# Three small parameter loads moved from GpSimd's queue to SyncE's, with three pairs of later loads merged

## The chip, the cores and the metric

The kernel runs on one core of a Trainium2 chip. The time is the device time of one execution in microseconds (us), as a median of several executions. The profile shows one execution in detail; its span, from the first recorded instruction to the last, is about 2 us shorter than the time.

Names used below: PE is the matmul engine, DVE the vector engine, ACT the scalar engine, POOL is GpSimd, SP is SyncE, which in this kernel does nothing but issue DMAs. SPq is SyncE's queue of issues.

## The reference, cut to what matters

```python
xn  = layernorm(x)                         # x: (1, 2048, 512), bf16
dt  = exp(log_dt)                          # 512 values each: log_dt, Lambda_re, Lambda_im
Lam_bar = exp(dt * (Lambda_re + 1j * Lambda_im))
ssm = scan over t of h = Lam_bar * h + B_bar xn[t], then 2 Re(C h) + xn * Dskip
glu = (silu(xn @ w1) * (xn @ w3)) @ w2     # w1, w3: 512 x 1792, w2: 1792 x 512
out = x + ssm + glu
```

The three parameter vectors, 512 bf16 values (1 KB) each, are the subject of the change.

## The kernel before

The 2048 rows of x are worked on in four blocks of 512. Of block 0 the normalised rows are transposed on PE; of blocks 1 to 3 by DMA transposes from SBUF to SBUF. The 14 gate tiles (128 columns of w1 and of w3 each) of block 0 begin as soon as the first weights are there. All weights, the x blocks and the transposes go through SyncE's queue in one order.

```python
    for c in range(2):                                         # x chunks 0 and 1, half each
        for eng, dsl in ((nc.sync, slice(0, D // 2)), (nc.scalar, slice(D // 2, D))):
            eng.dma_start(out=x_blk[0][:, c, dsl], in_=xv[:, c, dsl])
    nc.scalar.dma_start(out=x_blk[0][:, 3, :], in_=xv[:, 3, :])
    nc.sync.dma_start(out=x_blk[0][:, 2, :], in_=xv[:, 2, :])
    load_w(0, 2 * P)                                           # w1, then w3: gate tiles 0 and 1
    load_w(2 * P, 4 * P)                                       # tiles 2 and 3
    for i, src in enumerate((A_log_dt, A_Lambda_re, A_Lambda_im)):
        nc.gpsimd.dma_start(out=par_rows[i * NPT:(i + 1) * NPT, :], in_=src.rearrange("(t p) -> t p", p=P))

    def bulk_loads():
        ...                                                    # cut: one ACT write that holds the next load back
        load_w(4 * P, MID * P)                                 # tiles 4 to 7
        load_x(1)
        nc.sync.dma_start_transpose(out=bt_re, in_=A_B_re)
        nc.sync.dma_start_transpose(out=bt_im, in_=A_B_im)
        load_w(MID * P, 11 * P)
        load_w(11 * P, F)
        nc.sync.dma_start_transpose(out=ct_re, in_=A_C_re)
        nc.sync.dma_start_transpose(out=ct_im, in_=A_C_im)
        nc.sync.dma_start(out=w2_sb, in_=B_w2.rearrange("(t p) d -> p t d", p=P))    # 1.8 MB
        nc.sync.dma_start(out=dskip_row, in_=A_Dskip.partition_broadcast(P))
```

After these, SyncE issues block 1's four transposes (`xnT<-xn`), which PE needs when it begins block 1, near 39 us. Then come the loads of x blocks 2 and 3 (`late_loads`).

On PE the start of block 0 reads, shortened:

```python
            quarter(0, (0, 1), 2)      # 16 small matmuls: rows 0-127, tiles 0 and 1 (needs the first weight pair)
            pps = params_transpose()   # needs par_rows
            ...
            quarter(1, (0, 1))
            ln_first_transpose(2)
            quarter(0, (2,))           # needs the second weight pair
```

The loads from SyncE and ACT use eight completion semaphores in turn: the instruction listing shows each load, from the ninth on, waiting for the completion of the load eight places before it.

Of the kernel before, what the change touches and what calls it, by code (L numbers as in the profile page):

```python
# [16 lines left out]
P = 128  # L17
# [34 lines left out]
def kernel(  # L52
# [17 lines left out]
    nc = tc.nc  # L70
    _, S, D = A_x.shape
    F = B_w1.shape[1]
# [6 lines left out]
    NPT = PS // P  # L79
# [3 lines left out]
    MID = 8  # L83
# [30 lines left out]
    par_rows = const.tile([3 * NPT, P], BF16, name="par_rows")  # L114
# [15 lines left out]
    def load_w(f0, f1, eng1=nc.sync, eng3=nc.sync):  # L130
        eng1.dma_start(out=w1_sb[:, :, f0:f1], in_=w1v[:, :, f0:f1])  # L131
        eng3.dma_start(out=w3_sb[:, :, f0:f1], in_=w3v[:, :, f0:f1])

    def load_x(b, parts=1):
        n = CPB // parts
        for i in range(0, CPB, n):
            nc.sync.dma_start(out=x_blk[b][:, i:i + n, :], in_=xv[:, b * CPB + i:b * CPB + i + n, :])
# [4 lines left out]
    nc.scalar.dma_start(out=x_blk[0][:, 3, :], in_=xv[:, 3, :])  # L142
    nc.sync.dma_start(out=x_blk[0][:, 2, :], in_=xv[:, 2, :])  # L143
    load_w(0, 2 * P)
    load_w(2 * P, 4 * P)
    for i, src in enumerate((A_log_dt, A_Lambda_re, A_Lambda_im)):
        nc.gpsimd.dma_start(out=par_rows[i * NPT:(i + 1) * NPT, :], in_=src.rearrange("(t p) -> t p", p=P))

    def bulk_loads():
        nc.scalar.activation(out=w1_sb[:, 0, 4 * P:4 * P + 1], in_=rstd_all[:, 0:1], func=ACT.Copy)  # L150
        load_w(4 * P, MID * P)
        load_x(1)
        nc.sync.dma_start_transpose(out=bt_re, in_=A_B_re)
        nc.sync.dma_start_transpose(out=bt_im, in_=A_B_im)
        load_w(MID * P, 11 * P)
        load_w(11 * P, F)
        nc.sync.dma_start_transpose(out=ct_re, in_=A_C_re)
        nc.sync.dma_start_transpose(out=ct_im, in_=A_C_im)
        nc.sync.dma_start(out=w2_sb, in_=B_w2.rearrange("(t p) d -> p t d", p=P))
        nc.sync.dma_start(out=dskip_row, in_=A_Dskip.partition_broadcast(P))  # L160

    def late_loads():
        load_x(2)
        load_x(3, 2)


    ones = nc.const_aps.tensor(1.0, (P, TBLK), BF16)
# [276 lines left out]
    def glu(b):  # L444
# [25 lines left out]
        if b == 0:  # L470
# [13 lines left out]
            ln_stats(0, 0)  # L484
            ln_first_rstd(0)
            bulk_loads()
            ln_stats(0, 1)
            ln_first_rstd(1)
# [121 lines left out]
    bg.flush(("ln", 1))  # L610
    gate()
    late_loads()
    finish_c = [weight_c(pt) for pt in range(NPT)]
    res_tasks(0)
# [53 lines left out]
```

## Time and profile before

| | before |
|---|---|
| time, median of 6 runs | 213.28 us (212.97 to 214.24) |
| span of the profiled run | 211.6 us |
| PE busy | 207.6 us, 98% |
| granted PE clock | 0.999 |
| PE waits for the first w3 load until | 6.98 us |
| PE gap before block 1 | 0.22 us, until 39.40 us |

From the page of the kernel before, parts 1 and 4. The first line is busy time with its share and the number of instructions; the second is the chain of waits by engine.

```profile
PE 207.6 (98%) x1075; PEld 99.2 (47%) x1075; DVE 155.8 (74%) x186; ACT 116.5 (55%) x221; POOL 24.7 (12%) x50
...
PE 94%; DMA 2%; ACT 1%; SPq 1%; issue 0%; DVE 0%
```

PE bounds the kernel: only some 4 us of the span are not PE. A change of loads can win only where PE waits for a load.

From the timeline of the kernel before. The columns are start and duration in us, engine, line, operation, output and input, and count; the bracket is the idle time of the engine just before, and what ended it. These lines stand in order of time.

```profile
1.26 0.80 POOL L147 DMA_DIRECT2D par_rows<-in_A_log_dt_dram  x1 [0.83 <-POOLq L652]
2.60 0.51 SPq L132 DMA_DIRECT2D w_sb<-in_B_w_dram  x1
3.15 0.52 SPq L131 DMA_DIRECT2D w_sb<-in_B_w_dram  x1
3.72 0.51 SPq L132 DMA_DIRECT2D w_sb<-in_B_w_dram  x1
6.92 6.05 SPq L153 DMA_TRANSPOSE bt_re<-in_A_B_re_dram  x1
6.98 0.95 PE L481 MATMUL gu_ps<-xnT,w_sb 128*128 128x128 bf16 x14 [0.26 <-DMA w_sb<-in_B_w_dram]
9.11 0.61 PE L481 MATMUL bu_ps<-xnT,w_sb 128*128 128x128 bf16 x8
12.90 8.80 PE L451 MATMUL gu_ps<-xnT,w_sb 128*128 128x512 bf16 x40
27.46 9.25 SPq L223 DMA_TRANSPOSE xnT<-xn  x4
39.40 10.95 PE L451 MATMUL gu_ps<-xnT,w_sb 128*128 128x512 bf16 x50 [0.22 <-issue]
```

Read it so: the first w3 load is issued at 2.60, the second weight pair at 3.15 and 3.72. PE goes on at 6.98, when the first w3 load has landed. At 9.11 PE uses the second pair. Block 1's transposes are issued from 27.46 on, and PE begins block 1 at 39.40 after a short gap. The two gaps after the warm-up, 0.26 and 0.22 us, are all that the loads cost PE here.

### The profile page before, as it was taken

To read this page: it belongs to the slowest core of one execution; us is meant where nothing else is said; L and a number is where in the kernel's file an instruction comes from. 1 tells how busy PE (TensorE), PEld (TensorE's weight loads), DVE (VectorE), ACT (ScalarE), POOL (GpSimd) and SP (SyncE) were. 2 spreads that over 40 slices of the span, in tenths; PEclk is the share of its full clock that TensorE was granted. 3 is DMA by queue.
4 is the path that set the end of the run, shared out by engine and by line. 5 is a ranking of instruction groups with operands and counts; after the bars stand their busy time and mean duration, and the time that the engine had idled before them with its cause. 6 is when DMAs were issued, how large, how long until landed. Compare 5 with 4: busy or idle time off the path is not lost.

```text
span 211.6 us, 2823 instructions
## 1 busy us (share of the span) xinstructions
PE 207.6 (98%) x1075; PEld 99.2 (47%) x1075; DVE 155.8 (74%) x186; ACT 116.5 (55%) x221; POOL 24.7 (12%) x50
## 2 busy tenths in 40 slices
PE   8999999999999999999999999999999999999994
PEld 2864444444444444444444444444444444444464
DVE  4789799999918969899999897827999991121111
ACT  4699787699866864066666786036666630000000
POOL 7350299200000020000000012000000000000000
PEclk9999999999999999999999999999999999999999
DMA  5999999800000003500000001510000000100110
GB/s 160 326 237 283 251 297 166 248 0 0 0 3 0 0 0 77 99 25 0 0 0 5 0 0 25 124 50 3 0 2 0 3 0 0 50 25 28 36 40 25
DMA packets 27245, 13.68 MB, mean 65 GB/s; under 512 B 15840, under 2 KB 27232, under 8 KB 27232
## 3 DMA queue, kind: packets, MB, share of 16 engines
q1 hardware_dynamic: 26560, 13.21, 26.9%
q10 hardware_dynamic: 576, 0.30, 0.5%
q8 instruction: 8, 0.13, 0.2%
q14 instruction: 5, 0.04, 0.1%
q0 software_dynamic: 96, 0.00, 0.0%
HBM read 7.74 MB, written 2.10 MB: 46 GB/s over the span
## 4 chain that ended last, share of the span: by engine, by line
PE 94%; DMA 2%; ACT 1%; SPq 1%; issue 0%; DVE 0%
PE gu_ps L451 43%; PE y_ps L556 23%; PE y_ps L562 13%; PE bu_ps L379 12%; DMA w_sb<-in_B_w_dram 2%; PE gu_ps L481 2%; PE bu_ps L481 1%; ACT u L381 1%; SPq L141 0%; ACT tabe L346 0%; PE y_ps L219 0%; SPq L131 0%; SPq L143 0%; DVE o L567 0%; PE y_ps L280 0%
## 5 line engine op out<-in xcount | busy, mean ns | idle before, releaser
L451 PE MATMUL gu_ps<-xnT,w_sb 128*128 128x512 bf16 x424 | 92.3, 379 | 0.2 <-issue 0.2
L451 PEld LDWEIGHTS <-w_sb 128*128 128x128 bf16 x424 | 41.3, 98 | 50.3 <-issue 0.7
L556 PE MATMUL y_ps<-w_sb,hgT 128*128 128x512 bf16 (+2 forms) x252 | 50.4, 356 | 0.0
L461 ACT ACTIVATE u<-gu_ps 128x512 bf16<-128x512 f32 x55 | 33.2, 603 | 11.6 <-PE gu_ps L451 11.2
L460 ACT ACTIVATE g<-gu_ps 128x512 bf16<-128x512 f32 x55 | 33.1, 602 | 9.7 <-PE gu_ps L451 9.5
L567 DVE TENSOR_TENSOR o<-y_ps,xn 128x512 bf16<-128x512 f32 (+2 forms) x18 | 11.3, 629 | 35.8 <-PE y_ps L562 35.8
L556 PEld LDWEIGHTS <-hgT 128*128 128x128 bf16 x252 | 23.6, 98 | 25.2
L381 ACT ACTIVATE u<-bu_ps 128x512 bf16<-128x512 f32 x32 | 19.1, 597 | 24.5 <-PE bu_ps L379 24.5
L415 DVE TENSOR_TENSOR_SCAN u<-rho,h,u 128x512 bf16<-128x512 f32 x24 | 29.5, 1270 | 0.2
L467 DVE TENSOR_TENSOR hgT<-g,u 128x1024 bf16<-128x1024 bf16 x28 | 19.0, 682 | 6.6 <-ACT u L461 6.6
L562 PEld LDWEIGHTS <-h 128*128 128x128 bf16 x144 | 13.5, 98 | 14.3
L562 PE MATMUL y_ps<-ct_re,h 128*128 128x512 bf16 (+2 forms) x72 | 16.8, 356 | 0.0
L562 PE MATMUL y_ps<-ct_im,h 128*128 128x512 bf16 (+2 forms) x72 | 16.8, 356 | 0.0
L379 PE MATMUL bu_ps<-xnT,bt_re 128*128 128x512 bf16 x64 | 16.4, 379 | 0.1
L379 PE MATMUL bu_ps<-xnT,bt_im 128*128 128x512 bf16 x64 | 16.4, 379 | 0.0
L402 DVE TENSOR_TENSOR p<-u,tabe 128x2048 bf16<-128x2048 bf16 x8 | 9.8, 1222 | 3.5 <-ACT u L381 3.4
L252 POOL TENSOR_SCALAR acc<-acc 128x4 f32<-128x4 f32 x2 | 1.0, 497 | 80.8 <-ACT xn L251 80.8
L420 DVE TENSOR_TENSOR p<-u,tabe 128x2048 bf16<-128x2048 bf16 x8 | 9.8, 1224 | 0.2
L427 DVE TENSOR_TENSOR h<-h,p 128x2048 bf16<-128x2048 bf16 x8 | 9.8, 1223 | 0.2
L405 DVE TENSOR_TENSOR u<-u,tabe 128x2048 bf16<-128x2048 bf16 x8 | 9.8, 1222 | 0.2
L409 DVE TENSOR_TENSOR u<-u,p 128x2048 bf16<-128x2048 bf16 x8 | 9.8, 1224 | 0.1
L379 PEld LDWEIGHTS <-bt_re 128*128 128x128 bf16 x64 | 6.2, 98 | 7.8 <-issue 0.3
(92 smaller groups left out, 148.5 us busy)
## 6 DMA issues: line engine op xcount, KB each, us to landing
out_dram<-o SPq DMA_DIRECT2D x15, 128.0 KB, 1.7
w_sb<-in_B_w_dram SPq DMA_DIRECT2D x1, 1792.0 KB, 10.8
w_sb<-in_B_w_dram SPq DMA_DIRECT2D x4, 384.0 KB, 4.8
w_sb<-in_B_w_dram SPq DMA_DIRECT2D x4, 256.0 KB, 4.5
w_sb<-in_B_w_dram SPq DMA_DIRECT2D x2, 512.0 KB, 5.9
x_blk<-in_A_x_dram SPq DMA_DIRECT2D x2, 512.0 KB, 6.1
x_blk<-in_A_x_dram SPq DMA_DIRECT2D x2, 256.0 KB, 4.8
xnT<-xn SPq DMA_TRANSPOSE x12, 2.5
```

Source lines behind the costliest of these rows:

```text
L379: nc.tensor.matmul(out=ps, lhsT=bt[:, dt, pt * P:(pt + 1) * P], rhs=xnT_blk[b][:, dt, :], start=(dt == 0), stop=(dt == NDT - 1))
L381: nc.scalar.activation(out=u[:, j, ri, :], in_=ps, func=ACT.Copy)
L402: nc.vector.tensor_tensor(out=st["p"], in0=st["g"], in1=tabe[:, psl, 1:3, :], op=ALU.mult)
L405: nc.vector.tensor_tensor(out=st["g"], in0=st["g"], in1=tabe[:, psl, 0:1, :].to_broadcast(FULL), op=ALU.mult)
L415: nc.vector.tensor_tensor_scan(out=v, data0=rho[:, pt:pt + 1].to_broadcast([P, TBLK]), data1=v, initial=init, op0=ALU.mult, op1=ALU.add)
L451: nc.tensor.matmul(out=ps[:, tsl], lhsT=w[:, dt, f * P:(f + 1) * P], rhs=xnT[:, dt, tsl], start=(dt == 0), stop=(dt == NDT - 1))
L460: nc.scalar.activation(out=g16[:, f % 2, :], in_=g_ps, func=ACT.Silu)
L461: nc.scalar.activation(out=u16[:, f % 2, :], in_=u_ps, func=ACT.Copy)
L467: nc.vector.tensor_tensor(out=hgT[:, f - 1:f + 1, :], in0=g16, in1=u16, op=ALU.mult)
L556: nc.tensor.matmul(out=tiles[cl][:, dsl], lhsT=hg_blk[b][:, f, cl * P:(cl + 1) * P], rhs=w2_sb[:, f, dsl], start=(f == 0), stop=False)
L562: nc.tensor.matmul(out=tiles[cl][:, dsl], lhsT=h_blk[b][:, pt, ri, cl * P:(cl + 1) * P], rhs=ct[:, pt, dsl], start=False, stop=(ri == 1 an ...
L567: nc.vector.tensor_tensor(out=o[:, dsl], in0=tiles[cl][:, dsl], in1=xn_blk[b][:, cl, dsl], op=ALU.add)
```

## The change

The intent, as I read it, is to take GpSimd out of the loading and to let the parameters follow the weights that PE needs first. To keep the number of loads on SyncE, and with it the turns of the semaphores further on, four weight loads of 384 KB become two of 768 KB, and the two halves of x block 3 become one load.

```diff
     load_w(0, 2 * P)
+    for i, src in enumerate((A_log_dt, A_Lambda_re, A_Lambda_im)):
+        nc.sync.dma_start(out=par_rows[i * NPT:(i + 1) * NPT, :], in_=src.rearrange("(t p) -> t p", p=P))
     load_w(2 * P, 4 * P)
-    for i, src in enumerate((A_log_dt, A_Lambda_re, A_Lambda_im)):
-        nc.gpsimd.dma_start(out=par_rows[i * NPT:(i + 1) * NPT, :], in_=src.rearrange("(t p) -> t p", p=P))
 ...
-        load_w(MID * P, 11 * P)
-        load_w(11 * P, F)
+        load_w(MID * P, F)
 ...
-        load_x(3, 2)
+        load_x(3)
```

## The prediction

> **What bounds the kernel.** TensorE. The page of the kernel before has PE busy 207.6 of 211.6 us at a granted clock of 0.999; the chain of waits gives PE 94%, DMA 2%, ACT 1%. In the chain, the head is x and weight issues on SyncE until 2.60, then one DMA (the w3 half of gate tiles 0 and 1, 4.34 us to landing) until 6.94, then PE almost without a break to 208.9. In the timeline PE's gaps after its warm-up are 0.26 us at 6.7 (waiting for that w3 load) and 0.22 us at 39.2 (named "issue"; the fourth x transpose of block 1, issued near 35.5 and 3.6 us to landing, arrives near 39.1, so I take it for that). Together 0.48 us, 0.2% of the span: all that a change of loads can win in the middle.
>
> **What the change does.** The instruction listing shows PE, DVE and ACT with the same instructions in the same order.
> - Removed: three GpSimd issues (0.80, 0.53, 0.52 us, 1.26 to 3.10 in the timeline). GpSimd's constants come about 1.8 us earlier; nothing waits for them (ident is ready at 3.7, first used at 5.05).
> - Added: three SyncE issues behind the first weight pair, about 0.4 us each (x issues there took 0.40). The weights of tiles 2 and 3 then leave not at 3.15 and 3.72 but near 4.4 and, as the semaphores of these loads are handed round in turn and its slot now waits for the fourth x chunk (1.65 + 3.7 = 5.35), near 5.4. The w3 load of tiles 4 to 7 now waits for the first w1 load (landed 6.0), block 1's x for the first w3 load (6.9).
> - Also in the diff: four weight loads of 384 KB become two of 768 KB (two issues of about 0.5 us fewer, rows of 1536 B instead of 768 B), and two x loads become one.
>
> **What of it is critical.** The DMA engines are full from 2.5 us (9 tenths in every slice to 34 us, about 310 GB/s). At 4.4 us only about 0.55 of the first 1.05 MB has moved, so a later issue leaves no bubble: the tile-2 weights still land at about 8 to 8.8 us (before 7.65 and 8.7) and are wanted at 9.1. The first w3 load has less traffic mixed in and may land 0.2 to 0.5 us sooner, worth at most 0.26 us. The Trainium skill, "DMA: Bandwidth & Descriptors", "Issuing engines are not separate DMA queues", says that all queues run on the same 16 engines and a second issuer only saves issue time. Here that time is not on PE's path. The parameter rows now queue behind the weights and land near 7; PE wants them at 7.87, or near 7.6 if the head shortens: tight but probably no stall. Longer weight rows may bring block 1's transposes forward enough to close the 0.22 us gap.
>
> Sum: -0.25 (head) -0.15 (gap at 39) +0.1 (risk of a stall for tile 2's weights or the parameters) = -0.3 us.
>
> **Predicted:** 213.1 us, 80% range 212.4 to 214.0. Faster by over 2%: 0.01; within 2%: 0.98; slower by over 2%: 0.01.
>
> **What would show it.** Right: parameter issues on SyncE at 3.2 to 4.4; tile-2 weights issued near 4.4 and 5.4 yet landing before 9; PE's gaps at 6.7 and 39.2 smaller; PE busy 207 to 208. Wrong: PE waiting on DMA before the parameter transpose, or on w_sb at about 9 us; block 1's transposes landing later than 39.1.
>
> **What would make it wrong.** Small loads costing SyncE far more than 0.4 us each, or landing after 8 us; the semaphore waits leaving the DMA engines empty at 5 to 7 us, pushing every later load by 1 us or more. Even that costs 1 to 2 us, under 2%.

## More of the kernel before

From the windows view of the kernel before (columns: window, its length, PE busy time with number of instructions, granted clock, busy share of the DMA engines, GB/s moved):

```profile
5.50:7.00 1.50, 1.24 (x13) 1.00 1.14 310
7.00:13.00 6.00, 6.00 (x104) 1.00 1.14 318
13.00:24.00 11.00, 11.00 (x54) 1.00 1.12 259
```

## The result, and the profile after

Ratios are computed as the mean time of one kernel's runs over that of the other's in the same rounds, so they are not quite the ratio of the medians quoted. Executions over 1.5% slower than the fastest of the same kernel are left out of the means.

| | before | after |
|---|---|---|
| first comparison, medians of 6 and 6 runs | 213.28 us | 213.33 us (213.15 to 213.72) |
| ratio, 95% interval | | 1.0001 (0.9978 to 1.0023) |
| second comparison, one chip, 11 and 5 fast runs | 213.62 us | 213.49 us |
| ratio, 95% interval | | 0.9989 (0.9972 to 1.0007) |
| span of the profiled run | 211.6 us | 211.5 us |

The second comparison is the run e0_after_again below (its median with the slow run is 213.57 us). Both intervals contain 1: whatever the change does is smaller than about 0.3%.

The timeline of the changed kernel, the same places (its line numbers are one lower from the merged load on):

```profile
2.58 0.51 SPq L132 DMA_DIRECT2D w_sb<-in_B_w_dram  x1
3.13 0.45 SPq L146 DMA_DIRECT2D par_rows<-in_A_log_dt_dram  x1
3.62 0.26 SPq L146 DMA_DIRECT2D par_rows<-in_A_Lambda_re_dram  x1
3.93 0.29 SPq L146 DMA_DIRECT2D par_rows<-in_A_Lambda_im_dram  x1
4.27 0.40 SPq L131 DMA_DIRECT2D w_sb<-in_B_w_dram  x1
5.19 0.39 SPq L132 DMA_DIRECT2D w_sb<-in_B_w_dram  x1
6.69 0.95 PE L480 MATMUL gu_ps<-xnT,w_sb 128*128 128x128 bf16 x14 [0.30 <-DMA w_sb<-in_B_w_dram]
7.69 7.08 SPq L153 DMA_TRANSPOSE bt_re<-in_A_B_re_dram  x1
8.82 0.72 PE L480 MATMUL bu_ps<-xnT,w_sb 128*128 128x128 bf16 x8
12.72 8.80 PE L450 MATMUL gu_ps<-xnT,w_sb 128*128 128x512 bf16 x39
29.01 8.40 SPq L222 DMA_TRANSPOSE xnT<-xn  x4
39.32 10.95 PE L450 MATMUL gu_ps<-xnT,w_sb 128*128 128x512 bf16 x49 [0.33 <-DMA xnT<-xn]
```

PE goes on 0.29 us earlier after the first w3 load (6.69 against 6.98). The next line, eight matmuls on tile 2, takes 0.72 instead of 0.61 us: here PE waits for the second weight pair, which left later. At 12.72 it is still 0.18 us ahead. But block 1's transposes are issued 1.55 us later (29.01 against 27.46), and the gap before block 1 is larger, so that at 39.32 only 0.08 us of the lead is left. The last of the four, the one that PE waits for, landed only 0.12 us later than before (39.19 against 39.07 us), but PE now wanted it 0.2 us sooner. Most of the late issue is there as soon as SyncE is done with the transpose of bt_re, whose issue began 0.77 us later and took 7.08 instead of 6.05 us. In the chain of waits of the changed kernel the link before block 1 is no longer PE, but the fourth transpose:

```profile
36.20 2.99 DMA xnT<-xn
39.19 0.14 issue
39.32 2.75 PE gu_ps L450 x12
```

The windows view of the changed kernel:

```profile
5.50:7.00 1.50, 1.20 (x18) 1.00 0.84 219
7.00:13.00 6.00, 6.00 (x102) 1.00 1.12 310
13.00:24.00 11.00, 10.89 (x51) 1.00 1.14 235
```

The DMA engines move 219 GB/s between 5.5 and 7 us where they moved 310, and they do not make it up by 24 us. Rate difference times length gives about 0.14, 0.05 and 0.26 MB less for the three windows: the larger part is lost after 13 us, not in the dip. PE busy reads 206.4 us on this page against 207.6, but its trace holds 1057 matmul records instead of 1075, so that difference is one of missing records and says nothing.

### The profile page after: what moved, and what is told of

It reads as the page before. It is cut to its first block, busy times and chain, and to the rows that moved or that the text cites. A ratio compares the mean times of both kernels' runs of the same rounds, so it can differ in the third digit from the quotient of the medians.

```text
span 211.5 us, 2800 instructions
## 1 busy us (share of the span) xinstructions
PE 206.4 (98%) x1057; PEld 99.0 (47%) x1075; DVE 155.8 (74%) x186; ACT 116.5 (55%) x221; POOL 22.8 (11%) x47
## 4 chain that ended last, share of the span: by engine, by line
PE 81%; DVE 8%; ACT 3%; DMA 3%; SPq 1%; issue 1%; POOL 1%; DVEq 0%
PE gu_ps L450 34%; PE y_ps L555 23%; PE y_ps L561 13%; PE bu_ps L378 10%; DVE u L414 2%; DMA w_sb<-in_B_w_dram 2%; DMA xnT<-xn 1%; ACT g L459 1%; DVE stats L194 1%; ACT u L460 1%; PE gu_ps L480 1%; DVE hgT L466 1%; DVE xn L199 1%; ACT L510 1%; DVE u L408 1%
## 5 line engine op out<-in xcount | busy, mean ns | idle before, releaser
L378 PEld LDWEIGHTS <-bt_im 128*128 128x128 bf16 x64 | 6.3, 98 | 7.5
```

What stands on the lines that cost most here:

```text
L378: nc.tensor.matmul(out=ps, lhsT=bt[:, dt, pt * P:(pt + 1) * P], rhs=xnT_blk[b][:, dt, :], start=(dt == 0), stop=(dt == NDT - 1))
```

## The experiments

Four theories were to be told apart about the head, A or B for the earlier first weights, C or D for the lower DMA rate:

- A: the first w3 load lands earlier because the second weight pair, now later, is not mixed in with it.
- B: it lands earlier because the three GpSimd loads are gone.
- C: the small four-row loads hold up the DMA engines that serve them.
- D: the second pair's later issue leaves the DMA queue thin.

And one about the end: the arrival of block 1's transposes takes back what the head wins.

### e1_move_only: the move without the merges (one look)

```diff
     load_w(0, 2 * P)
+    for i, src in ...: nc.sync.dma_start(out=par_rows[...], ...)
     load_w(2 * P, 4 * P)
-    for i, src in ...: nc.gpsimd.dma_start(out=par_rows[...], ...)
```

> Only the parameter loads move to SyncE; the weight and x loads stay unmerged. If the move alone makes the changes seen in the head (both theories), the head is that of the changed kernel: first w3 load landed and PE going again at 6.7 us (before 6.98), DMA rate 5.5 to 7 us near 190 to 235 GB/s (before 306 to 312), the last load of block 1's transposes landing at 39.2 us or later. Two weight issues more than the changed kernel, so ct_re is issued about 1 us later than its 19.1 us, and the PE gap at 39 us is 0.33 us or up to 1 us more. If the merges hurt the queue instead, it is issued at or before 19 us.

The DMA rate from 5.5 to 7 us was 254 GB/s, above the expected range but well below the kernel before. The first weights came without a visible stop (16 matmuls in one group from 6.43 us). The ct_re load was issued at 20.44 us and the gap before block 1 was 1.14 us. So in this look the move alone goes with the dip and the late queue; the merges are not needed for either. How much they pay back is the question of the timed run further down.

### e3_params_second: parameters on SyncE behind the second weight pair (one look)

```diff
     load_w(0, 2 * P)
-    for i, src in ...: nc.sync.dma_start(out=par_rows[...], ...)
     load_w(2 * P, 4 * P)
+    for i, src in ...: nc.sync.dma_start(out=par_rows[...], ...)
```

> Parameter loads on SyncE, but behind the second weight pair. Theory A (the later weight pair makes the first w3 load land earlier, because less traffic is mixed in): the pair leaves at 3.1 and 3.7 again, so PE goes on at about 6.95 us as before. Theory B (the three GpSimd loads themselves had slowed the first weights): 6.7 us as in the changed kernel. Theory C (four-row loads in SyncE's rings hold up the DMA engines that serve them): the dip of the DMA rate (to about 200 GB/s) appears again, but later, about 6.5 to 8.5 us; theory D (the dip comes from the weight pair's late issue): no dip, 300 GB/s or more. Parameter rows land later, at 8 us or after, and PE waits for them before the parameter transpose (0 us before, up to 1 us now).

From its windows and its timeline:

```profile
5.50:7.00 1.50, 0.99 (x15) 1.00 1.13 338
...
6.88 0.95 PE L480 MATMUL gu_ps<-xnT,w_sb 128*128 128x128 bf16 x14 [0.51 <-DMA w_sb<-in_B_w_dram]
9.27 0.16 PE L279 MATMUL y_ps<-ident,par_rows 12*128 12x12 bf16 x1 [1.44 <-DMA par_rows<-in_A_Lambda_im_dram]
```

With the small loads on SyncE but the weight pair early, the rate stays at 338 GB/s, and from 7 to 13 us it is 316 GB/s. It sags to 297 and 266 GB/s in the half windows at 7.0 and 7.5 us (before: 300 and 296), which is not the dip to about 200 that C asked for: C is not borne out, D stands. But block 1's transposes were issued at 28.61 us, about 1.1 us later than before, without the dip: the low rate is not the only way to a late queue. PE went on at 6.88 us, between the two values expected, so this run does not tell A from B. It does show that the place of the parameters matters: behind the second pair they came so late that PE stood for 1.44 us, more than expected.

### e4_pool_plus_dummies: parameters on GpSimd, and three equal loads on SyncE into a tile that nobody reads (one look)

```diff
-    for i, src in ...: nc.sync.dma_start(out=par_rows[...], ...)
+    for i, src in ...: nc.gpsimd.dma_start(out=par_rows[...], ...)
+    dummy_rows = const.tile([3 * NPT, P], BF16, name="dummy_rows")
+    for i, src in ...: nc.sync.dma_start(out=dummy_rows[...], ...)
```

> The parameters stay on GpSimd and three equal loads into a tile that nobody reads go out on SyncE where the change put them. Theory A: PE goes on at about 6.7 us as in the changed kernel, since the second weight pair leaves late. Theory B: 6.95 us as before, since the GpSimd loads are there. Theories C and D both: the dip to about 200 GB/s at 5.5 to 7 us, ct_re issued near 19 us, the PE gap at 39 us about 0.3 us.

```profile
5.50:7.00 1.50, 1.11 (x17) 1.00 1.05 273
...
6.74 0.96 PE L483 MATMUL gu_ps<-xnT,w_sb 128*128 128x128 bf16 x14 [0.38 <-DMA w_sb<-in_B_w_dram]
```

PE went on at 6.74 us although the GpSimd loads were there: B cannot be the main cause. A small part for B is not excluded, as e3, with the early pair but no GpSimd loads, went on at 6.88 us, a little ahead of all four profiles that have both (6.98 to 7.57). The rate at 5.5 to 7 us was 273 GB/s, a dip, though a smaller one. The rest of the expectation was missed: ct_re was issued at 17.76 us instead of near 19, and there was no gap before block 1. With the same SyncE order as the changed kernel the queue was 1.3 us earlier, in spite of the dip. That told me how much of the queue's lateness is chance.

### e5_late_pair_no_small: the second pair held back by GpSimd, no small loads on SyncE (one look)

```diff
-    load_w(2 * P, 4 * P)
     for i, src in ...: nc.gpsimd.dma_start(out=par_rows[...], ...)
 ...
     nc.gpsimd.iota(iota_i, ...)
+    nc.gpsimd.memset(w1_sb[:, 0, 2 * P:2 * P + 1], 0.0)
     nc.gpsimd.tensor_copy(out=iota_f, in_=iota_i)
+    nc.gpsimd.memset(w3_sb[:, 0, 2 * P:2 * P + 1], 0.0)
+    load_w(2 * P, 4 * P)
```

(The merges of the changed kernel are in it too.)

> The parameters stay on GpSimd, no small load on SyncE; the second weight pair is held back by two GpSimd memsets to about 4.3 and 5.1 us (changed kernel 4.27 and 5.19). Merged loads as in the changed kernel. Theory C (small loads hold up DMA engines): no dip, at least 290 GB/s in 5.5 to 7 us, ct_re issued at or before 18.2 us, block 1's transposes landed before 39 us, PE gap at 39 us under 0.2 us. Theory D (late issue starves the DMA engines): dip to about 200 GB/s and ct_re at about 19 us. Theory A: PE goes on at about 6.7 us; theory B: 6.95 us.

```profile
5.50:7.00 1.50, 1.10 (x18) 1.00 0.96 267
...
6.70 0.95 PE L482 MATMUL gu_ps<-xnT,w_sb 128*128 128x128 bf16 x14 [0.40 <-DMA w_sb<-in_B_w_dram]
39.39 10.97 PE L452 MATMUL gu_ps<-xnT,w_sb 128*128 128x512 bf16 x50 [0.49 <-DMA xnT<-xn]
```

The pair left at 4.31 and 5.06 us. Everything that marks the changed kernel is here without a single small load on SyncE: PE going on at 6.70, a lower DMA rate (267 GB/s), ct_re at 19.48 us, a gap of 0.49 us before block 1. So the late issue of the second pair is enough for the lower rate, and of A and B it is A that fits e4 and e5 (first weights at 6.74 and 6.70 us with the GpSimd loads there). For D all fourteen profiles agree: 310 to 338 GB/s in the five where the pair left at 3.1 and 3.7 us, 219 to 273 in the nine where its first load left between 4.19 and 4.31. In the changed kernel the small loads act by taking SyncE's time (1.14 us) and by moving the turn of the semaphores, for which the second load of the pair waited another 0.5 us (4.67 to 5.19). That the low rate is what makes the queue late further on is not shown: e4 has the dip and a queue on time, e3 a late queue and no dip.

### e2_merge_only: only the merged loads

```diff
-        load_w(MID * P, 11 * P)
-        load_w(11 * P, F)
+        load_w(MID * P, F)
 ...
-        load_x(3, 2)
+        load_x(3)
```

> Only the merged loads, parameters still on GpSimd. Head as before: PE going on near 6.95 us, first full-width gate matmul at 12.9 us, SyncE reaching x of block 1 at 5.8 us. Theory: two issues fewer bring ct_re from 18.2 to about 17.2 us and block 1's transposes land about 0.5 to 1 us earlier, so no PE gap at 39 us, and the time is 0.2 to 0.5 us below before. Rival: the DMA engines, not the issues, set the pace there; then the gap stays 0.2 us or more and the time is that of before within 0.1 us.

Ratio 0.9993 (0.9952 to 1.0035), medians 213.80 against 213.72 us. Block 1's transposes were issued from 27.83 us (before: 27.46), so they were not issued sooner. The theory spoke of their landing, and the last one landed at 38.41 us, ahead of the first profile of the kernel before (39.07) but behind the second, b0 below (38.11): what the merges do to it cannot be read from one execution. The time is within 0.1 us of before, as the rival had it; the profiled execution had no gap before block 1, as the theory had it. PE also came late there: it waited 1.25 us for the first w3 load and went on at 7.57. In a kernel with the same head as before that wait had been 0.26 us.

### e1_move_again: the move without the merges, timed

> The move without the merges, timed, to see whether the 1.14 us gap at 39 us of the single look was chance. Theory: two more issues of 0.5 us stand ahead of the transposes in a queue that is just in time, so the time is 0.5 to 1 us above before (ratio 1.002 to 1.005) and the gap is over 0.6 us. Rival (chance of the DMA engines in one execution): the time is within 0.2 us of before and the gap differs from the first look by 0.5 us or more.

Ratio 0.9999 (0.9954 to 1.0043), medians 213.59 against 213.72 us. The profiled execution was the slowest of six (215.48 us; the others 213.23 to 213.89) and had a gap of 1.76 us:

```profile
31.89 7.44 SPq L223 DMA_TRANSPOSE xnT<-xn  x4
...
41.31 9.01 PE L451 MATMUL gu_ps<-xnT,w_sb 128*128 128x512 bf16 x41 [1.76 <-DMA xnT<-xn]
```

Both tests of the rival are met: the time is within 0.2 us of before, and the gap differs from the first look by 0.62 us. Of the theory only the gap came true, in the slowest execution of the six. PE went on at 7.23 us here, as late as with the early pair: the earlier first weights are a matter of chance too. The spans' means are 212.07 us here and 211.74 us before in the same rounds, so this kernel is 0.33 us longer inside the span (0.55 without the low-clock run of the kernel before) and 0.30 us shorter outside it (see the table under e0). Whether the merges are worth that is not settled, because its spans run from 211.4 to 213.7.

### e6_before_w2_late and e7_after_w2_late: the w2 and skip-row loads behind block 1's transposes

The same edit on the kernel before (e6) and on the changed kernel (e7):

```diff
     def bulk_loads():
 ...
-        nc.sync.dma_start(out=w2_sb, in_=B_w2.rearrange("(t p) d -> p t d", p=P))
-        nc.sync.dma_start(out=dskip_row, in_=A_Dskip.partition_broadcast(P))
     def late_loads():
+        nc.sync.dma_start(out=w2_sb, in_=B_w2.rearrange("(t p) d -> p t d", p=P))
+        nc.sync.dma_start(out=dskip_row, in_=A_Dskip.partition_broadcast(P))
```

> Kernel before, with the 1.8 MB w2 load and the skip row issued after block 1's four transposes instead of ahead of them. Theory (the arrival of those transposes gates PE at 39 us and its chance from run to run is the spread of the times): no PE gap at 39 us, the transposes land before 36 us, the median 0.2 to 0.5 us below before, and highest minus lowest under 0.5 us where before spreads over 1 us. Rival: nothing changes in time or spread.

> Changed kernel, with w2 and the skip row after block 1's transposes. Theory: no PE gap at 39 us, so the 0.18 us that the changed kernel is ahead at 12.7 us now reaches the end: 0.1 to 0.25 us below the kernel before with the same reordering, and 0.3 to 0.7 us below before. Rival: the head's gain is lost elsewhere and both reordered kernels are equal.

e6: ratio 0.9981 (0.9944 to 1.0018), median 213.48 us against 213.72. e7: ratio 0.9960 (0.9923 to 0.9996), median 213.02 us. From the timeline of e7, whose transposes were issued from 26.69 us:

```profile
26.69 5.71 SPq L222 DMA_TRANSPOSE xnT<-xn  x4
28.49 21.75 PE L450 MATMUL gu_ps<-xnT,w_sb 128*128 128x512 bf16 x100
```

A hundred matmuls run through the place where the gap had been; e6 shows the same. The spread of the times is 0.82 us in e6 and 0.51 us in e7, where that of before was 3.14 us in the same rounds (212.82 to 215.96). Most of that 3.14 is the one low-clock run; without it the spread is 1.39 us, and in the next call six runs of the unchanged kernel before spread by 0.40 us. So it is not shown that the transposes' arrival is a source of the spread, and e6 missed the expected 0.5 us. e6 has the other wait left: in its profile PE waited until 7.35 us for the first w3 load. e7 is 0.46 us below e6 in both mean and median, more than the 0.1 to 0.25 expected. The means of time and span, over the same runs, split that: 213.01 and 211.22 us for e7, 213.47 and 211.38 for e6, which is 0.16 us in the span (as expected of the head) and 0.30 us outside it (which I had not expected).

### b0_before_again and e0_after_again: both kernels once more on one chip

> The kernel before once more, for the chance of its two waits. Theory (both waits on loads are matters of chance in this kernel): the wait for the first w3 load is again somewhere between 0.2 and 1.3 us (seen in kernels with this head: 0.26, 1.25, 0.92), the gap at 39 us between 0 and 0.5 us, and the times spread by 1 us or more. Time minus span 1.96 to 2.15 us, as in all kernels with loads from GpSimd. Rival: head wait again 0.26 us and time within 0.3 us throughout.

> The changed kernel once more. Theory: the wait for the first w3 load is again 0.25 to 0.4 us, the tile-2 wait about 0.1 us, and the gap at 39 us is there and between 0.2 and 1 us; time minus span 1.79 us as in all kernels without loads from GpSimd. Ratio to before 0.997 to 1.001. Rival: no gap at 39 us and over 0.5 us faster than before.

```profile
5.50:7.00 1.50, 0.95 (x12) 1.00 1.11 317
7.02 0.95 PE L481 MATMUL gu_ps<-xnT,w_sb 128*128 128x128 bf16 x14 [0.57 <-DMA w_sb<-in_B_w_dram]
28.69 21.53 PE L451 MATMUL gu_ps<-xnT,w_sb 128*128 128x512 bf16 x99
```

These were from the kernel before; the following are from the changed kernel.

```profile
5.50:7.00 1.50, 0.97 (x15) 1.00 0.83 233
6.85 0.96 PE L480 MATMUL gu_ps<-xnT,w_sb 128*128 128x128 bf16 x14 [0.45 <-DMA w_sb<-in_B_w_dram]
39.54 10.73 PE L450 MATMUL gu_ps<-xnT,w_sb 128*128 128x512 bf16 x49 [0.42 <-DMA xnT<-xn]
```

The picture repeats: the changed kernel's rate dips again (233 GB/s, the kernel before 317), it goes on 0.17 us earlier at the first weights, and it has its gap before block 1, while the kernel before had none this time. The head wait of 0.45 us is a little over the expected 0.25 to 0.4. The kernel before spread less than I expected in these six runs (213.14 to 213.54), though its eleven baseline runs of the same call went from 213.10 to 214.00. Held against these baseline runs of the very same kernel its ratio is 0.9985 (0.9971 to 0.9999): an interval that excludes 1 for no change at all, so a difference of 0.15% must not be read here, and the changed kernel's 0.9989 is smaller than that. Time minus span, 1.93 us in its profiled execution and 2.02 in the mean, lies just under or in the expected 1.96 to 2.15. One of the changed kernel's six runs was slow.

Since each execution of these calls has its span recorded, time and span can be split. Means of the runs, in us:

| call | kernel | loads from GpSimd | runs | time | span | time minus span |
|---|---|---|---|---|---|---|
| 1 | before | yes | 11 | 213.83 | 211.74 | 2.09 |
| 1 | e2_merge_only | yes | 6 | 213.81 | 211.75 | 2.06 |
| 1 | e6_before_w2_late | yes | 6 | 213.47 | 211.38 | 2.09 |
| 1 | e1_move_again | no | 6 | 213.86 | 212.07 | 1.79 |
| 1 | e7_after_w2_late | no | 6 | 213.01 | 211.22 | 1.80 |
| 2 | before | yes | 11 | 213.59 | 211.53 | 2.06 |
| 2 | b0_before_again | yes | 6 | 213.32 | 211.30 | 2.02 |
| 2 | e0_after_again | no | 5 | 213.41 | 211.58 | 1.83 |
| 2 | e7_again | no | 6 | 212.83 | 211.05 | 1.78 |

Without its low-clock run the kernel before of call 1 has a time of 213.62 and a span of 211.52. Single executions lie between 1.90 and 2.15 with loads from GpSimd and between 1.74 and 1.85 without. e4 and e5, which keep the parameters on GpSimd, belong to the first group (1.98 and 2.10), e4 although it has SyncE's small loads too. So a program without GpSimd loads takes about 0.2 to 0.3 us less outside the recorded instructions. What is saved there, no view shows.

### e7_again, and e8_x2_on_act: can the head be made shorter still?

e8 is e7 with the third x chunk on ScalarE's queue, so that the first weight pair is issued 0.46 us earlier:

```diff
-    nc.scalar.dma_start(out=x_blk[0][:, 3, :], in_=xv[:, 3, :])
-    nc.sync.dma_start(out=x_blk[0][:, 2, :], in_=xv[:, 2, :])
+    nc.scalar.dma_start(out=x_blk[0][:, 2, :], in_=xv[:, 2, :])
+    nc.scalar.dma_start(out=x_blk[0][:, 3, :], in_=xv[:, 3, :])
```

> The changed kernel with w2 and the skip row behind block 1's transposes, once more, beside the others of this call. Theory: no gap at 39 us, 0.2 to 0.6 us below the changed kernel of this call, spread of its times 0.6 us or less. Rival: the first result (213.02 us) was chance and it equals the changed kernel.

> The kernel of e7 with the third x chunk issued on ScalarE's queue, so that the first weight pair leaves SyncE 0.46 us earlier (1.64 and 2.11). Theory: the first w3 load lands near 6.2 to 6.3 us and PE's wait for it (0.26 us in e7) goes; part comes back as a longer wait for tile 2's weights (0.1 us in e7) or for the parameters; 0.1 to 0.3 us below e7. Rival: the DMA engines set the landing and not the issue, the wait stays and the times are equal; or ScalarE, now 0.45 us later with its table load, delays the first normalisation and it is slower by 0.1 us or more.

e7_again: ratio 0.9962 (0.9948 to 0.9977), median 212.82 us, spread 0.52 us, no gap before block 1. By means it is 0.58 us below the changed kernel of the same call (212.83 against 213.41), of which 0.53 us are span. Against the kernel before its interval is clear of 1 in both calls, and its 0.38% is over twice what two sets of the same kernel differed by; against the changed kernel, by means 0.3%, no interval was computed. Both are far under the 2% that count as faster here.

e8: ratio 0.9968 (0.9953 to 0.9984), median 212.90 us, so equal to e7. The first w3 load was issued at 2.11 instead of 2.58 us, but took 4.6 us instead of 4.1 to 4.3 to land, at 6.73 us (e7: 6.67 and 6.92). The rival was right that the times are equal and that an earlier issue does not bring the load in earlier; that the DMA engines still have x in hand then is the likely reason, not a shown one. PE's wait did go, as the theory had it, but PE also came to these matmuls later (6.40 us, in e7 6.18 and 6.10), so nothing was won.

## Why the prediction was right or wrong

The time and the class were right: 213.1 us within 212.4 to 214.0, measured 213.33, and no difference beyond 2%. (213.1 fits 213.43 less 0.3; 213.43 is the median of the three runs in the first record of the kernel before.) The ground for that was right too: PE bounds the kernel, with two short gaps that loads can reach. But the range was wide enough for no change at all, and the gain of 0.3 us did not show: that the number fell close is partly luck, since one term had the wrong sign and another, of the same size, was not thought of. Of the prediction's own signs of being wrong two came: PE waited on w_sb at about 9 us, and the last of block 1's transposes landed after 39.1 (39.19, in e0 39.40).

| term of the sum | predicted | in the first pair of profiles | in the second pair |
|---|---|---|---|
| first w3 load earlier | -0.25 us | -0.29 (6.98 to 6.69) | -0.17 (7.02 to 6.85) |
| stall for tile 2's weights | +0.1 | +0.11 (0.61 to 0.72) | +0.07 (0.61 to 0.68) |
| gap before block 1 | -0.15 | +0.11 (0.22 to 0.33) | +0.42 (none to 0.42) |
| outside the span | not thought of | -0.29 (2.08 to 1.79) | -0.23 by means (2.06 to 1.83) |

- **Head, right in the main.** The issues came where predicted (parameters at 3.13 to 4.22 us, the second pair at 4.27 and 5.19, the latter held by the semaphore whose last load was the fourth x chunk, issued at 1.64 and 3.5 us to landing). The pair landed at 8.36 and 9.09 us, the second a little after the 9 us that the prediction had set. e4 and e5 point to the later pair as what makes the first weights land earlier. The small loads cost SyncE 1.14 us together (3.13 to 4.27), about the 1.2 predicted. In four profiles with the early pair (before, b0, e2, e6) PE went on at 6.98, 7.02, 7.57 and 7.35 us; in four of the changed kernel with or without late w2 (after, e0, e7, e7_again) at 6.69, 6.85, 6.72 and 6.96. By those means, 7.23 and 6.80, the head's gain is 0.4 us; with e1_move_again, which has the same head and went on at 7.23, it is 0.3. The ranges overlap, so its size is rough.
- **"A later issue leaves no bubble", the step that failed.** I took the DMA engines for full from 2.5 us on and the queue for deep enough; that the engines might run empty at 5 to 7 us I had named only as what would make it wrong. The rate at 5.5 to 7 us fell from 310 and 317 to 219 and 233 GB/s, and e5 shows the fall without small loads, e3 small loads without the fall. In the same profiles the whole queue ran late: block 1's transposes were issued at 29.01 and 29.47 us instead of 27.46 and 27.58. That the one makes the other is not shown (e3 and e4, and the windows after 13 us, speak against it as the whole cause).
- **"Longer weight rows may bring block 1's transposes forward", wrong in sign as a consequence.** e2 has the longer rows alone; its transposes were issued no earlier (27.83 us), and the last landed between those of the two profiles of the kernel before. In the changed kernel they landed as late as PE wanted them or later, so the gap grew instead of closing and took back the head's gain. e7 takes w2 out of their way and the gap is gone, together with 0.53 us of span against the changed kernel.
- **Outside the span, not foreseen.** I counted the GpSimd loads as costing nothing, since nothing in the span waited for them. All kernels without them have about 0.2 to 0.3 us less between span and time. In the second comparison this is all that is left of a gain: the spans are equal (211.53 and 211.58 us; b0, once more the kernel before, has 211.30).

So the time stood still because a gain in the head and one outside the span were given back, before block 1 as far as the profiles show where; e7, which removes that loss, brings the gain out. The account does not close to a tenth: the terms of the first pair of profiles sum to -0.36 us, but that profile of the kernel before was of a slow execution (213.73 us against a median of 213.28), and the medians are equal. The main point of the Trainium skill, "DMA: Bandwidth & Descriptors", "Issuing engines are not separate DMA queues", that the loads share the DMA engines whichever engine starts them, no view used here tests. It also calls the issue time usually small relative to the DMA, and so it was for each small load (0.26 to 0.45 us; the weight loads of 256 KB took 3.8 to 4.1 us to land); but three in a row, 1.14 us, put in front of a load that is wanted soon, went with a thinner queue.

What stays open: why the queue's lateness varies so much from one execution to the next. SyncE's issue of the bt_re transpose took 5.86 to 6.05 us in before, b0, e2 and e6, but 7.08, 7.70, 7.59, 8.87 and 7.82 us in after, e0, both e1 and e5, 6.49 to 6.87 in e7, e7_again and e3, and then again 6.10 and 6.07 in e4 and e8, which have the late pair as well. In all fourteen profiles this issue ended 0.15 to 0.32 us before the load just ahead of it, block 1's x, landed (13.29 us before, 14.93 after): it seems to follow the progress of the loads and not to be a cost of its own. The lateness is already in the first weight load of tiles 4 to 7, which landed at 10.2 to 10.6 us where it was issued at 4.8 to 4.9, and at 11.5 to 12.8 where it was issued at 5.5 to 6.3, but at 10.6 again in e4 and e8 (issued at 5.61 and 5.75). A late issue there, behind a late pair or, as in e3, behind the small loads alone, makes a late queue likelier but does not fix it. What the merges are worth beside the move is not settled either.

## What to carry to other kernels

A lead that loads win early is worth nothing if PE meets a later load that has not come forward too; look for the next place at which PE and a load arrive together (here 39 us) and move what stands in the queue ahead of that load and is wanted much later (w2, first used near 70 us). A small load can cost what it pushes back and not what it moves: ask which large load stands behind it, and whether the DMA queue runs thin meanwhile. And where two waits on DMAs are just in time, one profile is one draw of them: repeat both kernels before giving a tenth of a microsecond a cause.

## What the Trainium skill lacked or had wrong

- "DMA: Bandwidth & Descriptors", "Issuing engines are not separate DMA queues": it speaks of sequencer time as the only thing that a second issuer saves. It has nothing on a cost outside the instructions: programs with loads from GpSimd took 1.90 to 2.15 us between span and time, those without 1.74 to 1.85. "Runtime: NRT & Kernel Launch" is the page for what lies around a kernel, but gives no such difference either.
- The same page, "Anatomy of one DMA — SWDGE (gpsimd) path", fits the time of a GpSimd load as about 2.0 us plus bytes over bandwidth. The three 1 KB loads from GpSimd took 2.8, 3.6 and 3.7 us to land here, beside the loads of x and weights, so the fit is too low for this case.
- The same page gives no measured time of an issue on SyncE of this chip. Here it was 0.37 to 0.58 us for most loads of 128 partitions (1.08 and 1.37 us for two of the kernel before) and 0.45, 0.26 and 0.29 us for the three loads of four rows of the changed kernel.
- No page says how much the DMA engines vary from one execution to the next: the same first w3 load of the same head took 4.3, 4.4, 4.7 and 4.9 us to land.
